# Attention inside a fused attention and MoE kernel: both key tiles kept apart in the first 16 units, and x divided by the softmax sums in place of the weights

## The chip, the cores and the metric

The kernel runs on one core of one Trainium2 chip. The metric is the device time of one launch in microseconds (us). The kernel before took 806.68 us (median of three runs, 804.89 to 807.85).

## The reference

Windowed attention with four sink keys, then a gated two-layer MLP ("MoE" in the names) over all tokens:

```
scores = q @ k.T / sqrt(64);  keep = (key < n_sink) or (0 <= query - key < window)
a = softmax(where(keep, scores, -1e9));  a = exp(s - max) / (sum + 1e-9)
x = (a @ v) gathered over 8 heads                      # 3072 tokens x 512
out = (sigmoid(x @ w_gate) * (x @ w_val)) @ w_out      # 512 -> 1536 -> 512
```

Batch 4, 8 heads, 768 tokens, head size 64; n_sink is 4 and window is 128, read at run time; the MoE weights come as float64 and are decoded on the chip into a high and a low float32r part.

## The kernel before

Attention runs in 96 units. A unit is one head of one batch over T = 2 query tiles of 128 tokens; units 0 to 7 are the heads of tiles 0 and 1 of batch 0, units 8 to 15 those of tiles 2 and 3, and so on. With a window of 128, a query tile sees the key tile before it and its own, and the four sink keys; the k array holds, after each 128 keys, the four sink keys again (KW = 132 columns per key tile). The first 16 units (`u < PLAIN`, L31) multiply in plain float32 from the loaded q, k and v; the others split their operands into high and low parts.

A unit before (`attend`, L691): TensorE (PE) makes the scores of a query tile, 132 columns for tile 0 and 260 for the rest: the key tile before, sinks, own key tile (`qk`, L733). VectorE (DVE) merges the two key tiles by COPY_PREDICATED with a triangle mask, since of each pair of keys 128 apart a query uses exactly one (`top`, L742), and makes the masked, negated scores and their minimum in one custom instruction over 132 columns. ScalarE (ACT) takes exp with the row sum (`exp`, L750). Then the sum gets 1e-9 (`guard`), its reciprocal is taken, the 128 weights of a row are multiplied by it on whichever of POOL (GpSimd), ACT or DVE the planner picks (L772), and the four sink weights go, multiplied, into `psk` (L791). PE transposes the merged weights (`turn`, L809), ACT copies them to SBUF, and two AFFINE_SELECTs on POOL unmerge them into two key tiles (`split`, L815). PE multiplies with v (`pv`, L871). After eight heads `join` (L927) adds the sink part (`sk`, `vsp`) to x and splits x into XH and XL, on which the MoE part (`feed_part`, L1090) works.

The order of every engine's instructions is written by a planner (`Plan.run`, L287): an event simulation with a cost in ns per operation, priorities (unit number; MoE matmuls have a late one), buffers per tag, and due times for the 36 weight decodes (L1160). Where PE has nothing ready before 130 us of the planner's time and its activity is under a floor, the planner puts a filler matmul (`warm`, L648, identity times identity, 128 columns, into m0); in the trace this is `m<-ident`. What is planned is a fixed order: on the chip each engine goes through it in line, and fillers are executed whether or not PE has to wait.

Of the kernel before, what the change touches and what calls it, by code (L numbers as in the profile page):

```python
# [20 lines left out]
NS = 4  # L21
# [411 lines left out]
def kernel(  # L433
# [124 lines left out]
    assert NR == 32  # L558
    VSP = Fixed(const.tile([3 * NR, H // 2, 2 * D], F32R, name="vsp"))
# [6 lines left out]
    VAL, MASKS, IDENT = Fixed(val), Fixed(am), Fixed(ident)  # L566
    nums = tile([128, 10], I32, "nums", 1)
# [59 lines left out]
    def later_masks():  # L627


        rel, relm, inm = mk()[:, 0:128], mk()[:, 432:560], mk()[:, 560:688]  # L630
        snk, inp = mk()[:, 400 : 400 + NS], mk()[:, 688 : 688 + NS]
        V.tensor_scalar(out=inm, in0=relm, scalar1=win, scalar2=None, op0=ALU.is_lt)
        V.tensor_scalar(
            out=inp, in0=rel[:, 0:NS], scalar1=128.0, scalar2=win, op0=ALU.add, op1=ALU.is_lt
        )
        V.tensor_tensor(out=inp, in0=snk, in1=inp, op=ALU.is_gt)
        for i, x in ((1, inp), (2, snk)):
            low(am[i][:, 0:128], inm)
            low(am[i][:, 128:KW], x)

# [16 lines left out]
    plan.op(0, [("V", 1200, later_masks)], [VAL, mk], [(MASKS, 1), (MASKS, 2)])  # L657
# [32 lines left out]

    def attend(u, b, h, t0, T, XR, XS, PSK):  # L691
# [7 lines left out]
        plain = u < PLAIN  # L699
# [4 lines left out]
        load(u, b, h, t0, T, prev, L, vraw, qkT, plain)  # L704
        kk2, qq2 = [(qkT, 0), (qkT, 4)], [(qkT, 2), (qkT, 6)]
        if plain:
            pairs = ((qT, kTf),)
            qk_reads, qk_ns = [qkT], 4
        else:
            qs = tile([128, W], F32R, "qs", BUFS["qs"])  # L710
            kh = tile([128, L * KW], F32R, "kh", BUFS["kh"])
            kl = tile([128, L * KW], F32R, "kl", BUFS["kh"])
            copy(u, W, qs, qT, qq2, [qs])
            copy(u, L * KW, kh, kTf, kk2, [kh])
            rest(
                u, W, lambda: qs()[D:128], lambda: qT()[D:128], lambda: qs()[D:128],
                qq2 + [qs], [qs],
            )
            rest(u, L * KW, kl, kTf, kh, kk2 + [kh], [kl])
            pairs = (qs, kh), (qs, kl)  # L720
            qk_reads, qk_ns = [qs, kh, kl], 2

        if h == 0:
            PSK[0] = tile([128, T, H, NS], F32, "psk", BUFS["psk"])
# [3 lines left out]
        for t in range(T):  # L728
            sc = tile([128, 512], F32, "a", BUFS["a"], ps)
            first = t0 + t == 0  # L730
            n = KW if first else KW + 128

            def qk(t=t, sc=sc, n=n):  # L733
                s0 = max(t + prev - 1, 0) * KW
                K = D if plain else 128
                for i, (qq, kk) in enumerate(pairs):
                    PE.matmul(
                        sc()[:, 0:n], lhsT=qq()[0:K, t * 128 : t * 128 + 128],
                        rhs=kk()[0:K, s0 : s0 + n], start=i == 0, stop=i == len(pairs) - 1,
                    )  # L740
# [14 lines left out]

            plan.op(u, [("PE", 10 + qk_ns * mac(n), qk)], qk_reads, [sc, (P, t)], busy=0.5 if plain else 0.9)
# [34 lines left out]
        def sink_weights(E):  # L791
            return lambda: E.tensor_tensor(
                out=psk()[:, 0:T, h], in0=P()[:, 0:T, 128:KW],
# [10 lines left out]
        Z = 1 if plain else 2  # L804
        wt = tile([128, 2, T, 2, 128], F32 if plain else F32R, "wt", BUFS["w"])
        w = lambda: wt()[:, 0:Z]
# [8 lines left out]
        def split():  # L815
            f = 1 - prev
            if T > f:
                G.affine_select(
                    out=w()[:, :, f:T, 0], in_=f32(w())[:, :, f:T, 1],
                    pattern=[[0, Z], [0, T - f], [-1, 128]], compare_op=ALU.is_gt, fill=0.0,  # L820
# [4 lines left out]
                pattern=[[0, Z], [0, T], [1, 128]], compare_op=ALU.is_ge, fill=0.0, base=0,  # L825
# [7 lines left out]
        if not plain:  # L833
            plan.op(
                u, [("V", vec(W), lambda: V.tensor_tensor(
                    out=w()[:, 1, :, 1], in0=tpv(), in1=w()[:, 0, :, 1].bitcast(F32),
                    op=ALU.subtract,
                ))],
                [tp, (wt, 0)], [(wt, 1)],
            )  # L840
        plan.op(u, [("G", 1100.0 if plain else 1400.0, split)], [], [wt])

        if plain:
            vhl = vraw
        else:
            vhl = tile([128, L, 2 * D], F32R, "vhl", BUFS["vhl"])
            copy(u, L * D, lambda: vhl()[:, :, 0:D], vraw, [vraw], [(vhl, 0)])
            rest(
                u, L * D, lambda: vhl()[:, :, D : 2 * D], vraw, lambda: vhl()[:, :, 0:D],
                [vraw, (vhl, 0)], [(vhl, 1)],  # L850
            )

        acc = None if plain else tile([128, 512], F32, "a", BUFS["a"], ps)
# [3 lines left out]
        if plain and h % 2 == 0:  # L857
            XR[0] = tile([128, 512], F32, "a", BUFS["a"], ps)
        xr = XR[0]
        M = D if plain else 2 * D  # L860


        blocks = []
        for l in range(L):
            tl = l - prev
            n = 128 if (tl < 0 or tl == T - 1) else 256
            blocks.append((-n, l, max(tl, 0) * 128, 0 if tl < 0 else tl * 256 + 128, n))
        blocks.sort()
        assert blocks[0][-1] == W

        def pv():  # L871
            a = (xr()[e : e + D] if plain else acc())[:, 0 : Z * W].rearrange("p (z x) -> p z x", z=Z)
# [8 lines left out]
        if plain:  # L881
            plan.op(
                u, [("PE", sum(5 + 4 * n / 2.4 for *_, n in blocks), pv)], [vhl, wt], [(xr, h % 2)]
            )
            if h % 2:
                plan.op(
                    u, [("A", act(W, True), lambda: A.copy(out=xs()[:, c], in_=xr()[:, 0:W]))], [xr],
                    [(xs, (c, 0)), (xs, (c, 1))],
                )
        else:  # L890
            low = tile([D, W], F32, "low", BUFS["small"])
            plan.op(
                u, [("PE", sum(mac(2 * n) for *_, n in blocks), pv)],
                [vhl, wt], [acc, low, (xs, (c, h % 2))],
            )
            plan.op(
                u, [("A", act(W, True), lambda: A.copy(out=low(), in_=acc()[D:128, 0:W]))], [acc], [low]
            )
            if u < ADDG:
                low2 = tile([D, W], F32, "low2", BUFS["small"])  # L900
                plan.op(
                    u, [("A", act(W, True), lambda: A.copy(out=low2(), in_=acc()[0:D, 0:W]))], [acc],
                    [low2],
                )
                plan.op(
                    u, [("G", pool(W), lambda: G.tensor_tensor(
                        out=low(), in0=low2(), in1=low(), op=ALU.add
                    ))],
                    [low2], [low],
                )  # L910
            else:
                plan.op(
                    u, [("V", vec(W), lambda: V.tensor_tensor(
                        out=low(), in0=acc()[0:D, 0:W], in1=low(), op=ALU.add
                    ))],
                    [acc], [low],
                )
            plan.op(
                u, [("V", vec(W), lambda: V.tensor_tensor(
                    out=xs()[e : e + D, c], in0=acc()[0:D, W : 2 * W], in1=low(), op=ALU.add  # L920
                ))],
                [acc, low], [(xs, (c, h % 2))],
            )
        if h == H - 1:
            join(u, b, t0, T, XS, psk)

    def join(u, b, t0, T, XS, psk):  # L927
# [3 lines left out]
        sk = tile([3 * NR, W], F32R, "sk", BUFS["sk"])  # L931

        def turn():
            for t in range(T):
                PE.transpose(
                    out=ts()[0:NR, t * 128 : t * 128 + 128],
                    in_=psk()[:, t].rearrange("p h s -> p (h s)"), identity=ident,
# [13 lines left out]
        )  # L951
        runs = [[0]]
# [5 lines left out]
        for i, xs in enumerate(XS):  # L958
# [15 lines left out]
            )  # L974
            for run in runs:
# [191 lines left out]
    for b in range(B):  # L1167
        t0 = 0
        for T in AT[b]:
            XR, XS, PSK = [None], [], [None]  # L1170
            for h in range(H):
                attend(u, b, h, t0, T, XR, XS, PSK)
# [81 lines left out]
```

## Time and profile before

| | |
|---|---|
| median of the runs | 806.68 us |
| the profiled execution's own time | 806.56 us |
| its span, first to last instruction | 804.9 us |
| PE busy | 787.0 us (98%) |
| DVE, ACT, POOL busy | 511.5, 415.7, 437.5 us |
| DMA | 94.35 MB, mean 117 GB/s |

Matmuls are pipelined and their ends are modelled, so one row's duration overlaps the next row's start; what a matmul costs in a stream is read from start to start. A float32 matmul has two records in the trace, so the 108 fillers are 216 records. The page's busy share of PE holds the fillers, which do no work for the result.

### The profile page before, as it was taken

What the parts mean: (1) busy time and instruction counts of PE and PEld (TensorE: products, weight loads), DVE (VectorE), ACT (ScalarE), POOL (GpSimd) and SP (SyncE); (2) the same over time, 40 slices, a digit from 0 to 9 for tenths busy, and PEclk for the clock granted to TensorE, in tenths of its full rate; (3) what the DMA queues carried; (4) which work ended last, traced back from release to release, by engine and by line L of the source; (5) the groups of instructions that cost most, each with busy time, mean ns of one, the idle gap of its engine ahead of it and who ended that gap; (6) DMA issues with size and microseconds to landing.
All of it is one profiled execution on the core that took longest, in us unless ns stands there. A gap on an engine that the chain in (4) does not pass through costs nothing. (4 is left out here: it accounts for less than half of the span.)

```text
span 804.9 us, 14932 instructions
## 1 busy us (share of the span) xinstructions
PE 787.0 (98%) x4618; PEld 715.3 (89%) x4618; DVE 511.5 (64%) x1560; ACT 415.7 (52%) x1173; POOL 437.5 (54%) x609
## 2 busy tenths in 40 slices
PE   9999999998999999999999999999999999999995
PEld 6787888977999989999999999999999999999994
DVE  6587798989888898989971388885861321111110
ACT  4677778787777776767760157663740210011001
POOL 4475689887678776766762267673751221121111
PEclk9999999999999999999999999999999999999998
DMA  4657676774735443544541134353311121112111
GB/s 138 173 172 210 181 223 203 235 237 130 207 107 153 127 133 93 149 110 122 141 113 58 43 113 129 106 129 107 96 44 42 48 71 40 50 43 78 40 40 56
DMA packets 98422, 94.35 MB, mean 117 GB/s; under 512 B 43168, under 2 KB 77984, under 8 KB 98336
## 3 DMA queue, kind: packets, MB, share of 16 engines
q1 hardware_dynamic: 98336, 93.32, 40.7%
q8 instruction: 39, 0.64, 0.3%
q14 instruction: 47, 0.39, 0.2%
HBM read 83.85 MB, written 9.44 MB: 116 GB/s over the span
## 5 line engine op out<-in xcount | busy, mean ns | idle before, releaser
L487 POOL TENSOR_TENSOR gl<-th,gh 128x384 fp32r<-128x384 f32 (+1 forms) x72 | 69.4, 963 | 197.0 <-DVE gh L487 184.8
L487 DVE SCALAR_TENSOR_TENSOR th<-th,m 128x384 f32<-128x384 f32 (+1 forms) x108 | 54.4, 504 | 180.3 <-PE m L487 178.6
L487 ACT ACTIVATE th<-m 128x384 f32<-128x384 f32 (+1 forms) x108 | 48.9, 453 | 208.2 <-PE m L487 206.8
L487 POOL TENSOR_SCALAR_AFFINE_SELECT wt<-wt 128x512 fp32r<-128x512 f32 (+3 forms) x192 | 119.8, 624 | 45.9 <-DVE wt L487 27.7
L487 PE MATMUL m<-XH,wvh 128*128 128x384 f32 (+1 forms) x432 | 140.0, 324 | 0.3 <-ACT th L487 0.3
L487 PE MATMUL m<-XH,wgh 128*128 128x384 f32 (+1 forms) x432 | 139.8, 324 | 0.0
L487 PE MATMUL m<-XH,wvl 128*128 128x384 f32 (+1 forms) x432 | 137.4, 318 | 0.0
L487 PE MATMUL m<-XH,wgl 128*128 128x384 f32 (+1 forms) x432 | 137.4, 318 | 0.0
L487 PE MATMUL m<-XL,wgh 128*128 128x384 f32 (+1 forms) x432 | 137.3, 318 | 0.0
L487 PE MATMUL m<-XL,wvh 128*128 128x384 f32 (+1 forms) x432 | 137.3, 318 | 0.0
L487 PE MATMUL o<-woh,gh 128*128 128x512 f32 x276 | 113.0, 410 | 1.0 <-DVE total L1202 1.0
L487 PE MATMUL o<-woh,gl 128*128 128x512 f32 x276 | 109.7, 397 | 1.3 <-DVE gl L487 0.6
L487 PE MATMUL o<-wol,gh 128*128 128x512 f32 x276 | 108.9, 395 | 2.0 <-DMA wol<-wol_d 2.0
L487 ACT ACTIVATE P<-P,negm_all 128x132 f32<-128x132 f32 x192 | 77.0, 402 | 31.5 <-DVE negm_all L487 28.7
L487 PEld LDWEIGHTS m<-XH,wvh 128*128 128x128 f32 x432 | 81.4, 188 | 3.3 <-issue 0.5
L487 PEld LDWEIGHTS m<-XH,wgh 128*128 128x128 f32 x432 | 81.5, 189 | 1.9 <-issue 0.3
L487 PEld LDWEIGHTS m<-XL,wgh 128*128 128x128 f32 x432 | 81.5, 189 | 1.5
L487 PEld LDWEIGHTS m<-XL,wvh 128*128 128x128 f32 x432 | 81.5, 189 | 1.4
L487 PEld LDWEIGHTS m<-XH,wvl 128*128 128x128 f32 x432 | 81.4, 188 | 0.0
L487 PEld LDWEIGHTS m<-XH,wgl 128*128 128x128 f32 x432 | 81.4, 188 | 0.0
L487 DVE CUSTOM_DVE_ANT_0 P<-a,am 128x132 f32<-128x132 f32 x192 | 56.0, 294 | 16.7 <-PE a L487 7.6
L487 PEld LDWEIGHTS o<-woh,gl 128*128 128x128 f32 x276 | 52.1, 189 | 15.8 <-DVE gl L487 1.8
(114 smaller groups left out, 1657.2 us busy)
## 6 DMA issues: line engine op xcount, KB each, us to landing
wol<-wol_d SPq DMA_DIRECT2D x108, 256.0 KB, 2.8
qkT<-in_k_dram SPq DMA_DIRECT2D x120, 99.0 KB, 2.6
qkT<-in_q_dram SPq DMA_DIRECT2D x176, 64.0 KB, 2.5
wst<-in_moe_w_gate_dram SPq DMA_DIRECT2D x12, 512.0 KB, 4.2
wst<-in_moe_w_val_dram SPq DMA_DIRECT2D x12, 512.0 KB, 4.4
wst<-in_moe_w_out_dram SPq DMA_DIRECT2D x12, 512.0 KB, 3.7
vraw<-in_v_dram SPq DMA_DIRECT2D x64, 96.0 KB, 2.4
out_dram<-w SPq DMA_DIRECT2D x23, 256.0 KB, 2.3
```

Source lines behind the costliest of these rows:

```text
L487: return lambda *a, **kw: tc.keep_in_program_order(op(*a, **kw))
```

## The change

For units 0 to 15 a new function `attend_plain` takes the place of the plain branches of `attend`:

- The two key tiles of a query tile stay apart. The mask-and-minimum instruction and exp work on 260 columns (132 for tile 0), with masks `am2` that hold the triangle; they are made at the start by eight more DVE instructions. COPY_PREDICATED and the AFFINE_SELECTs of these units go.
- PE transposes both halves: one or two transposes per query tile in place of one; each query tile's result is copied by an instruction of its own, on ACT or DVE.
- The weights are not divided. The row sums of 8 heads are collected in `psk` (40 columns in place of 32), and the sink weights are copied there unscaled. In `join`, 1e-9 is added and the reciprocal taken once for all heads, the transposed reciprocals are copied to `rt` (8 x 256), and for each half of x PE spreads them over 64 rows per head with four float32 matmuls (`spread`), by which DVE multiplies x.
- The planner's costs for these float32 matmuls change: `60 + 0.97 * n` for a score matmul (before `10 + 4 * mac(n)`), `10 + n` per block of `pv` (before `5 + 4 * n / 2.4`).

```diff
+    def attend_plain(u, b, h, t0, T, XR, XS, PSK):
...
+            def top(t=t, sc=sc, n=n, m=m):
+                V.tensor_tensor_reduce(
+                    out=P[t]()[:, 0:n], in0=sc()[:, 0:n], in1=m()[:, 0:n], op0=ALU.add,
+                    op1=ALU.min, scale=-SCALE, scalar=3.0e38, accum_out=negm_all[:, u, t : t + 1],
+                )
+            def exp(t=t, n=n):
+                A.activation(
+                    out=P[t]()[:, 0:n], in_=P[t]()[:, 0:n], func=AF.Exp,
+                    bias=negm_all[:, u, t : t + 1], scale=-1.0,
+                    accum_out=psk()[:, t, NR + h : NR + h + 1],
+                )
...
+            plan.op(u, [("PE", 60 + 0.97 * n, qk)], [qkT], [sc, (TURN, 0)], busy=0.5)
...
+                for y in range(y0, 2):
+                    c = KW if y > y0 else 0
+                    PE.transpose(
+                        out=tp()[:, (2 * t + y) * 128 : (2 * t + y) * 128 + 128],
+                        in_=P[t]()[:, c : c + 128], identity=ident,
+                    )
...
+                def spread(i=i, rpv=rpv):
+                    for k in range(4):
+                        e = k % 2 * D
+                        PE.matmul(
+                            rpv()[e : e + D, k // 2],
+                            lhsT=ident[0:H, 4 * i + k : 4 * i + k + 1].to_broadcast([H, D]),
+                            rhs=rt(), start=True, stop=True,
+                        )
+                plan.op(u, [("PE", 4 * (10 + W), spread)], [rt, IDENT], [rp], busy=0.5)
+                plan.op(
+                    u, [("V", vec(2 * W), lambda rpv=rpv, xs=xs: V.tensor_tensor(
+                        out=xs(), in0=rpv(), in1=xs(), op=ALU.mult
+                    ))],
+                    [rp], [xs],
+                )
```

Where instructions moved, three places. First PE around the products with v (`vraw`) of units 4 and 5: in the order before, with the weights in tiles P, and `m<-ident` the fillers:

```order
L487 MATMUL a_430<-ident,P_362 128x128 x2
L487 MATMUL m_90<-ident 128x128
L487 MATMUL a_435<-qkT_303 128x132
L487 MATMUL a_443<-qkT_303 128x260
L487 MATMUL a_447<-ident,P_385 128x128 x2
L487 MATMUL m_90<-ident 128x128
L487 MATMUL a_456<-qkT_364 128x132
L487 MATMUL m_90<-ident 128x128 x2
L487 MATMUL a_470<-qkT_364 128x260
L487 MATMUL m_90<-ident 128x128 x3
L487 MATMUL a_487<-wt_437,vraw_403 64x256
L487 MATMUL a_487<-wt_437,vraw_403 64x128
```

The order now around the products of units 2 and 3, where the weights lie in the tiles kh and kl:

```order
L487 MATMUL m_90<-ident 128x128
L487 MATMUL a_339<-qkT_269 128x132
L487 MATMUL m_90<-ident 128x128 x4
L487 MATMUL o_353<-wt_342,vraw_302 64x256
L487 MATMUL o_353<-wt_342,vraw_302 64x128
L487 MATMUL o_357<-ident,kh_308 128x128
L487 MATMUL a_360<-qkT_269 128x260
L487 MATMUL o_357<-ident,kl_325 128x128 x2
L487 MATMUL m_90<-ident 128x128 x3
L487 MATMUL a_382<-qkT_282 128x132
L487 MATMUL m_90<-ident 128x128 x2
L487 MATMUL o_353<-wt_365,vraw_333 64x256
```

Fillers stand in both, and each unit has three transposes in place of two. Over the whole order there are 108 fillers before and 100 now (73 and 65 of them ahead of the first MoE matmul), 192 transposes of weights before and 216 now.

Second, PE at the first join (`psk` is turned, then the sink part is added), before:

```order
L487 MATMUL a_559<-ident,psk_246 32x128 x2
L487 MATMUL a_565<-qkT_450 128x260
L487 MATMUL a_570<-wt_527,vraw_494 64x256
L487 MATMUL a_570<-wt_527,vraw_494 64x128
L487 MATMUL m_90<-ident 128x128 x3
L487 MATMUL a_588<-qkT_450 128x260
L487 MATMUL m_90<-ident 128x128 x3
L487 MATMUL a_570<-wt_563,vraw_505 64x256
L487 MATMUL a_570<-wt_563,vraw_505 64x128
L487 MATMUL a_612<-sk_568,vsp 128x256 x2
L487 MATMUL a_617<-sk_568,vsp 128x256 x2
```

And now, where `low` holds the transposed reciprocals and the matmuls into 64x256 are `spread`:

```order
L487 MATMUL a_557<-ident,psk_239 40x128 x2
L487 MATMUL m_90<-ident 128x128 x4
L487 MATMUL a_575<-wt_537,vraw_516 64x256
L487 MATMUL a_575<-wt_537,vraw_516 64x128 x2
L487 MATMUL a_581<-sk_561,vsp 128x256 x2
L487 MATMUL a_589<-low_570,ident 64x256 x4
L487 MATMUL a_598<-sk_561,vsp 128x256 x2
L487 MATMUL m_90<-ident 128x128 x6
L487 MATMUL a_611<-low_570,ident 64x256 x4
```

Eight float32 matmuls of 256 columns have come in at each of the two joins of the plain units.

Third, DVE ahead of the first mask-and-minimum instruction (ISA), before and now (`vhl` holds the new masks `am2`, `am_86` is the mask of tile 0):

```order
L487 TENSOR_TENSOR wst_156<-wst_156 128x4
L487 TENSOR_SCALAR am_87<-wst_156 128x128
L487 TENSOR_SCALAR am_87<-wst_156 128x4
L487 TENSOR_SCALAR am_88<-wst_156 128x128
L487 TENSOR_SCALAR am_88<-wst_156 128x4
L487 ISA P_212,negm_all<-a_192,am_86 128x132
```

```order
L487 SCALAR_TENSOR_TENSOR vhl_203<-wst_156,am_87 128x128
L487 COPY vhl_203<-am_87 128x4
L487 TENSOR_SCALAR vhl_203<-wst_156 128x128
L487 TENSOR_TENSOR vhl_203<-vhl_203,am_87 128x128
L487 TENSOR_SCALAR am_88<-wst_156 128x128
L487 TENSOR_SCALAR am_88<-wst_156 128x4
L487 SCALAR_TENSOR_TENSOR vhl_210<-wst_156,am_88 128x128
L487 COPY vhl_210<-am_88 128x4
L487 TENSOR_SCALAR vhl_210<-wst_156 128x128
L487 TENSOR_TENSOR vhl_210<-vhl_210,am_88 128x128
L487 ISA kh_231,negm_all<-a_192,am_86 128x132
```

Eight instructions now stand ahead of the first softmax instruction on DVE.

## Rows read from the trace of the kernel before

**Rows 1.** Busy time in stretches of the span. Columns: from:to in us, length, then PE busy (x instructions), PE weight loads, DVE, ACT, POOL, granted TensorE clock, DMA share, GB/s.

```profile
0.00:25.00 25.00, 23.28 (x85) 17.43 (x85) 13.99 (x63) 10.70 (x31) 9.62 (x19) 1.00 0.50 141
25.00:52.00 27.00, 27.00 (x164) 20.15 (x163) 18.42 (x68) 20.22 (x56) 17.13 (x25) 1.00 0.59 170
52.00:95.00 43.00, 42.37 (x269) 34.13 (x269) 32.06 (x99) 31.71 (x80) 27.37 (x40) 1.00 0.72 208
95.00:200.00 105.00, 98.67 (x687) 89.02 (x688) 96.66 (x218) 81.54 (x193) 89.91 (x98) 1.00 0.67 201
200.00:420.00 220.00, 219.01 (x1375) 204.17 (x1374) 192.56 (x649) 158.21 (x499) 159.34 (x252) 1.00 0.49 132
420.00:795.00 375.00, 373.56 (x2042) 348.53 (x2041) 157.77 (x465) 111.53 (x315) 134.08 (x179) 1.00 0.24 70
```

**Rows 2.** PE in order of time, shortly before the first MoE matmul, and the transpose with which the second join begins. Columns: start, duration in us, operation, shape, count of records.

```profile
38.59 1.38 PE L487 MATMUL m<-ident 128*128 128x128 f32 x10
39.80 0.38 PE L487 MATMUL a<-ident,P 128*128 128x128 f32 x2
40.02 0.39 PE L487 MATMUL m<-ident 128*128 128x128 f32 x2
40.34 1.14 PE L487 MATMUL a<-qkT 64*128 64x260 f32 x4
41.41 1.38 PE L487 MATMUL m<-ident 128*128 128x128 f32 x10
42.63 0.38 PE L487 MATMUL a<-ident,P 128*128 128x128 f32 x2
...
50.59 1.60 PE L487 MATMUL m<-ident 128*128 128x128 f32 x12
51.96 0.36 PE L487 MATMUL m<-XH,wgh 128*128 128x256 f32 x1
...
89.73 0.38 PE L487 MATMUL a<-ident,psk 128*32 128x128 f32 x2 [0.64 <-DVE psk L487]
```

**Rows 3.** The same view a little later: the product with v of a unit with three key tiles (one matmul of 256 columns and two of 128, six records), the MoE matmul behind it, and two transposes with the MoE matmul behind them.

```profile
54.27 1.08 PE L487 MATMUL a<-wt,vraw 128*64 128x256 f32 x6
55.29 0.39 PE L487 MATMUL m<-XH,wvh 128*128 128x256 f32 x1
...
56.11 0.38 PE L487 MATMUL a<-ident,P 128*128 128x128 f32 x2
56.24 0.36 PE L487 MATMUL m<-XH,wgh 128*128 128x256 f32 x1
```

**Rows 4.** The same view near the start, with the time at which PE's pace changes.

```profile
5.36 3.30 PE L487 MATMUL a<-qkT 64*128 64x132 f32 x8 [0.17 <-DMA qkT<-in_q_dram]
...
12.54 1.67 PE L487 MATMUL a<-qkT 64*128 64x132 f32 x4
14.14 1.65 PE L487 MATMUL m<-ident 128*128 128x128 f32 x6
15.58 0.64 PE L487 MATMUL a<-ident,P 128*128 128x128 f32 x2
...
18.90 1.54 PE L487 MATMUL a<-wt,vraw 128*64 128x256 f32 x4
...
21.52 1.54 PE L487 MATMUL a<-wt,vraw 128*64 128x256 f32 x4
23.00 1.61 PE L487 MATMUL m<-ident 128*128 128x128 f32 x10
...
24.98 0.93 PE L487 MATMUL a<-qkT 64*128 64x132 f32 x4
25.84 0.49 PE L487 MATMUL m<-ident 128*128 128x128 f32 x2
```

**Rows 5.** Groups of instructions over the whole span, shapes kept apart. Columns: count, busy us, mean ns of one, idle time before them and what ended it.

```profile
L487 ACT ACTIVATE P<-P,negm_all 128x132 f32<-128x132 f32 x192 | 77.0, 402 | 31.5 <-DVE negm_all L487 28.7 <-POOL wt L487 0.9 <-DVE rs L487 0.8
L487 DVE CUSTOM_DVE_ANT_0 P<-a,am 128x132 f32<-128x132 f32 x192 | 56.0, 294 | 16.7 <-PE a L487 7.6 <-ACT wgh L487 1.3 <-DVE a L487 0.2
L487 ACT ACTIVATE P<-P,rs 128x128 f32<-128x128 f32 x125 | 46.3, 397 | 19.6 <-DVE rs L487 17.9 <-DVE bad L1188 0.8
L487 DVE COPY_PREDICATED a<-tri,a 128x128 f32<-128x128 int32 x160 | 45.6, 285 | 8.2 <-PE a L487 7.2 <-DVE rs L487 0.3
L487 PE MATMUL m<-ident 128*128 128x128 f32 x216 | 39.3, 318 | 2.3 <-POOL ident masks.py:199 1.4 <-ACT th L487 0.9
L487 DVE TENSOR_TENSOR xr<-a,xr 128x512 f32<-128x512 f32 x24 | 16.4, 685 | 2.9 <-PE a L487 2.6
L487 POOL TENSOR_SCALAR_AFFINE_SELECT wt<-wt 128x256 f32<-128x256 f32 x24 | 12.2, 507 | 5.1 <-ACT wt L487 4.0
L487 DVE RECIPROCAL rs<-rs 128x2 f32<-128x2 f32 x96 | 15.2, 159 | 7.1 <-POOL rs L487 5.6
L487 ACT COPY wt<-a 128x256 f32<-128x256 f32 x16 | 6.0, 375 | 3.8 <-PE a L487 3.6
```

**Rows 6.** DVE in order of time at the start: the last masks and the first mask-and-minimum instruction.

```profile
5.32 0.35 DVE L487 SCALAR_TENSOR_TENSOR wst<-wst,val 128x128 f32<-128x128 f32 x1
...
6.67 0.50 DVE L487 TENSOR_SCALAR am<-wst 128x128 f32<-128x128 f32 x4
7.08 0.29 DVE L487 CUSTOM_DVE_ANT_0 P<-a,am 128x132 f32<-128x132 f32 x1
```

More of the change, by code (lines that the diff above doesn't have):

```diff
@@ L566 @@
     VAL, MASKS, IDENT = Fixed(val), Fixed(am), Fixed(ident)
+    TURN = Fixed(None)
+    am2 = [None] + [tile([128, PW], F32, "vhl", BUFS["vhl"]) for _ in range(2)]
     nums = tile([128, 10], I32, "nums", 1)
@@ L703, in attend @@
         kTf = lambda: qkT()[:, W : W + L * KW]
-        load(u, b, h, t0, T, prev, L, vraw, qkT, plain)
+        load(u, b, h, t0, T, prev, L, vraw, qkT, False)
         kk2, qq2 = [(qkT, 0), (qkT, 4)], [(qkT, 2), (qkT, 6)]
[L706 to L721, printed above, removed]
+        qs = tile([128, W], F32R, "qs", BUFS["qs"])
+        kh = tile([128, L * KW], F32R, "kh", BUFS["kh"])
+        kl = tile([128, L * KW], F32R, "kl", BUFS["kh"])
+        copy(u, W, qs, qT, qq2, [qs])
+        copy(u, L * KW, kh, kTf, kk2 + [TURN], [kh])
+        rest(
+            u, W, lambda: qs()[D:128], lambda: qT()[D:128], lambda: qs()[D:128],
+            qq2 + [qs], [qs],
+        )
+        rest(u, L * KW, kl, kTf, kh, kk2 + [kh, TURN], [kl])
+        pairs = (qs, kh), (qs, kl)
         if h == 0:
-            PSK[0] = tile([128, T, H, NS], F32, "psk", BUFS["psk"])
+            PSK[0] = tile([128, T, NR], F32, "psk", BUFS["psk"])
         psk = PSK[0]
@@ L754, in exp @@
                 )
-            plan.op(u, [("PE", 10 + qk_ns * mac(n), qk)], qk_reads, [sc, (P, t)], busy=0.5 if plain else 0.9)
+            plan.op(u, [("PE", 10 + 2 * mac(n), qk)], [qs, kh, kl], [sc, (P, t)], busy=0.9)
             plan.op(
@@ L832, in attend @@
         )
[L833 to L853, printed above, removed]
+        plan.op(
+            u, [("V", vec(W), lambda: V.tensor_tensor(
+                out=w()[:, 1, :, 1], in0=tpv(), in1=w()[:, 0, :, 1].bitcast(F32),
+                op=ALU.subtract,
+            ))],
+            [tp, (wt, 0)], [(wt, 1)],
+        )
+        plan.op(u, [("G", 1400.0, split)], [], [wt])
+        vhl = tile([128, L, 2 * D], F32R, "vhl", BUFS["vhl"])
+        copy(u, L * D, lambda: vhl()[:, :, 0:D], vraw, [vraw], [(vhl, 0)])
+        rest(
+            u, L * D, lambda: vhl()[:, :, D : 2 * D], vraw, lambda: vhl()[:, :, 0:D],
+            [vraw, (vhl, 0)], [(vhl, 1)],
+        )
+        acc = tile([128, 512], F32, "a", BUFS["a"], ps)
         if h % 4 == 0:
@@ L856, in attend @@
         xs, c = XS[-1], h // 2 % 2
[L857 to L869, printed above, removed]
+        blocks = blocks_of(T, prev)
         def pv():
-            a = (xr()[e : e + D] if plain else acc())[:, 0 : Z * W].rearrange("p (z x) -> p z x", z=Z)
+            a = acc()[:, 0 : 2 * W].rearrange("p (z x) -> p z x", z=2)
             for i, (_, l, c0, r0, n) in enumerate(blocks):
@@ L880, in attend @@
         e = (h % 2) * D
-        if plain:
-            plan.op(
[L883 to L894, printed above, removed]
+        low = tile([D, W], F32, "low", BUFS["small"])
@@ new lines, in attend @@
+        plan.op(
+            u, [("PE", sum(mac(2 * n) for *_, n in blocks), pv)],
+            [vhl, wt], [acc, low, (xs, (c, h % 2))],
+        )
+        plan.op(
+            u, [("A", act(W, True), lambda: A.copy(out=low(), in_=acc()[D:128, 0:W]))], [acc], [low]
+        )
+        if u < ADDG:
+            low2 = tile([D, W], F32, "low2", BUFS["small"])
+            plan.op(
+                u, [("A", act(W, True), lambda: A.copy(out=low2(), in_=acc()[0:D, 0:W]))], [acc],
+                [low2],
@@ L895, in attend @@
             )
             plan.op(
-                u, [("A", act(W, True), lambda: A.copy(out=low(), in_=acc()[D:128, 0:W]))], [acc], [low]
-            )
[L899 to L917, printed above, removed]
+                u, [("G", pool(W), lambda: G.tensor_tensor(
+                    out=low(), in0=low2(), in1=low(), op=ALU.add
+                ))],
@@ L924, in attend, with join @@
         if h == H - 1:
             join(u, b, t0, T, XS, psk)
-    def join(u, b, t0, T, XS, psk):
+    def join(u, b, t0, T, XS, psk, plain=False):
         W, g, vs = T * 128, b * NT + t0, VSP
@@ L931, in join @@
         sk = tile([3 * NR, W], F32R, "sk", BUFS["sk"])
+        nr = NR + H if plain else NR
         def turn():
@@ L951, in join @@
         )
+        if plain:
+            rt = tile([H, W], F32, "low", BUFS["small"])
+            plan.op(
+                u, [("A", act(W, True), lambda: A.copy(out=rt(), in_=ts()[NR:nr, 0:W]))], [ts], [rt]
+            )
         runs = [[0]]
```

145 lines of the change are left out of this document (129 added, 16 removed).

## The prediction, made before the changed kernel was run

> **What bounds the kernel now.** I read the busy times by stretch first [rows 1]. From 200 to 795 us PE is busy for 592.6 of 595 us: whatever is late at 200 us is late at the end, and whatever has come earlier is gained. So the change, which ends in the second join at about 95 us, is worth what it does to the time at which PE is through with the attention of units 0 to 15 and the MoE matmuls that lie between. Two stretches come before that. From 95 to 200 us DVE is busy for 96.7 of 105 us and POOL for 89.9, with most of the weight decodes in them, and PE idles 6.3 us. From 0 to 95 us DVE has 64.5, ACT 62.6 and POOL 54.1 us of work: none of them is full.
>
> The question is then what sets the pace of the first 95 us, and the order of PE in time answers it [rows 2]. From 25 to 52 us PE is busy for 27.00 of 27 us [rows 1], and that is not waiting in disguise: five fillers from 38.59 to 39.80 us are 0.242 us apart, five from 41.41 to 42.63 us 0.244, six from 50.59 to 51.96 us 0.228. If PE waited for a transpose's weights, the fillers ahead would be through sooner or the last would be stretched unevenly. The planner put a filler wherever it thought PE idle, but its costs for the other engines are long, so on the chip they are ready when PE comes. In the first 95 us PE's own line, fillers included, is the bound. The reader is to see that an engine with 16% of its work in fillers can still be the one that everybody waits for.
>
> **The change part by part.** PE first, since its line is the sum.
>
> Spread: 16 float32 matmuls of 256 columns, eight per join. No row has this shape. The nearest is the product with v, also float32 into 64 partitions: 512 columns in 55.29 - 54.27 = 1.02 us, 2.0 ns a column [rows 3], so 0.51 us each and 8.2 us in all. The score matmuls agree: two of 260 columns take 41.41 - 40.34 = 1.07 us [rows 2]. That they read 8 rows and not 128 should not matter, as 64 rows (scores) and 128 (products) cost the same by column. The planner reckons 4 * 266 = 1.06 us for four of them, where the rows say 2.04. Upper end 8.6 us (score rate), lower end half, 4.1 us, if two that write different halves of the partitions could run together; I take 8.2, the row.
>
> The Trainium skill has a rule that speaks for the lower end ("TensorE: Matmul & The Clock Gate", Part 3, on packing small matmuls): matmuls placed on different column groups of the array can be in flight at the same time, and three of them gave 2.38 times the speed there. The four of a spread alternate between partitions 0 and 64, so by it the sum would be some 4 us lower. In this trace no two neighbours write different halves, so it shows neither.
>
> Transposes: 24 more (216 for 192). Two take 0.22 us ahead of a filler [rows 2] and 0.13 us ahead of an MoE matmul [rows 3]: 1.6 to 2.6 us, I take 2.1.
>
> Fillers: 8 fewer (100 for 108) at 0.242 us [rows 2]: -1.9 us. In the trace they are the 216 records of the group [rows 5]. Up to about 23 us, where PE runs at half pace, both orders hold about as many, so the full-pace price stands.
>
> Scores and products with v keep their number and shapes: 0. That the planner now thinks them nearly half as long (a score matmul of 260 columns 312 ns, where the row has 535) makes it believe PE idle too early; it only moves them, and the fillers it adds for that are in the count.
>
> So PE's line gets longer by 8.2 + 2.1 - 1.9 = 8.4 us.
>
> The other engines lose work. DVE: 24 COPY_PREDICATED at 285 ns, 6.8 us, and 16 reciprocals at 159 ns, 2.5 us [rows 5]; it gains 128 columns in 24 mask-and-minimum instructions (0.13 us each by the slope between 132 columns, 294 ns, and 512 columns, 685 ns [rows 5]), 3.2 us, four multiplications of x at 685 ns, 2.7 us, and the masks. POOL loses 24 selects at 507 ns, 12.2 us [rows 5], and the eight smaller ones of tile 0. ACT, POOL and DVE together lose 32 scalings (397 ns on ACT, at most 12.7 us) and gain 16 copies of at most 375 ns and 24 longer exps (402 ns before; the same 0.13 us more, 3.1 us). All of this lies beside PE's line in a stretch where the three are two thirds busy; I cost it at nothing. If that cover were gone, the extra DVE and ACT work would cost up to 6 us, and the removed work would give back more: that is the first rival.
>
> Masks: the eight new DVE instructions stand ahead of the first mask-and-minimum instruction, which starts at 7.08 us; one of 128x128 with three inputs takes 0.35 us and four plain ones start to start 0.41 us [rows 6], so eight take at most 2.8 us. Behind it waits exp, then PE's first transpose. But PE now has 784 columns of scores (4.1 ns a column at half pace: 392 in 14.14 - 12.54 us [rows 4]) and six fillers ahead of that transpose, 3.2 + 2.9 = 6.1 us from its first score at 5.36 us [rows 4], until 11.5; DVE is through with the first mask at 7.08 + 2.8 + 0.3 = 10.2 and ACT at 10.6. Cost 0; uncovered 2.8 us. (A filler at half pace is 0.48 us: three from 14.14 to 15.58 us [rows 4].)
>
> Join: reciprocal, turn, copy to `rt`, spread, multiplication now stand between `psk` and XH, some 3 us more of a chain. PE fills it with six fillers, the other spread, transposes and scores, and the MoE work that is issued by the product of unit 17 is the same in both orders (174 matmuls into m, 30 into o). Cost 0; uncovered up to 3 us a join.
>
> Against this, waits of PE may shrink. What can go is the 0.6 us of idle before 95 us and the 6.3 us to 200 us [rows 1]; the latter follow DVE's work on decodes and on units 16 and up, which the change leaves (12 of 36 decodes stand ahead of the 32nd mask-and-minimum instruction before, 13 now), but PE arrives later at it. Between 0 and 7 us, I take 2.5.
>
> Sum: 8.4 - 2.5 = +5.9 us on the profiled execution's 806.56 us (0.12 us under the median of the runs): 812.5 us.
>
> **The rivals.**
>
> One, faster: the other engines set the pace of the first 95 us and PE's even fillers deceive me. Then a unit's chain loses a reciprocal (0.16 us), a scaling (0.40) and two selects (1.01) [rows 5], some 1.6 us; with two units in flight that is 0.8 us a unit, 12.5 us in 16 units, and PE's 8.4 us lie partly in its waits. 806.6 - 12.5 = 794, with half of the PE work paid 798 us. For it: 18 of 63 fillers are gone by the product of unit 7. Against it: 27.00 of 27 us. It decides if PE is seen to wait between fillers.
>
> Two, no change: the spreads run in pairs. 4.1 + 2.1 - 1.9 - 2.5 = +1.8, 808.4 us. For it nothing but the alternating halves; against it that no row shows such an overlap.
>
> Three, slower still: PE stays at half pace longer. At 12.54 us 392 score columns took 1.60 us, at 24.98 us 0.86 [rows 4]; the granted clock reads 1.00, the upper level of 2.4 GHz, in both stretches [rows 1], so the pace is read from the starts. Ahead of the rise PE ran two products and fillers without a score matmul between (18.90 to 23.00 us). In the new order scores and transposes stand between, and the next such run (four fillers and a product) comes some 8 us later: each us costs half, +4 us, 816.5 us.
>
> **How the numbers follow.** Forecast 0.50, faster 0.17, paired spreads 0.20, late clock 0.13. The likeliest is 812.5 us, its own range 809 to 816 (spreads at 8.2 to 8.6, transposes 1.6 to 2.6, waits 0 to 5.5). The range of 8 in 10 is 803 to 819 us: below it lies most of rival one, above it a late clock with an uncovered join. Half a per cent, 4 us, is about what a measurement of this kernel can tell from no change. Faster by more than that (under 802.6): rival one, 0.17. Within: rival two and the low end of the forecast, 0.20 + 0.08. Slower (over 810.7): the rest of the forecast and rival three, 0.42 + 0.13 = 0.55.
>
> **What would show it.** Right: spreads 0.5 us apart, 1.0 us for two; fillers still evenly 0.24 us apart between 25 and 50 us; the second `psk` transpose, at 89.73 us before [rows 2], some 5 to 9 us later; DVE, ACT and POOL less busy before 95 us with no gain from it; from 200 us on as before. Wrong: a second `psk` transpose before 88 us (rival one), spreads 0.25 us apart (two), score matmuls at 4 ns a column after 25 us (three), or a middle stretch (the first split score to the last decode) that got shorter by more than 5 us, since then the other engines' order, which I took as unchanged there, decided.

## The result, and the profile after

The changed kernel took 809.59 us (median) against 804.89 us for the kernel before: the ratio is 1.0065 with a 95% interval of 1.0039 to 1.0090, that is 5.2 us slower (3.1 to 7.2; the two medians differ by 4.7). Of the 13 executions three lie far above the others (816, 830 and 1006 us), where all 70 of the kernel before stayed under 809 us; none of the three was profiled, and this ratio and those below leave out executions more than 1.5% above the quickest of their kernel.

The profiled execution took 809.59 us, its span is 807.8 us. The page's line of busy times of the changed kernel:

```profile
PE 791.2 (98%) x4658; PEld 716.3 (89%) x4658; DVE 511.8 (63%) x1538; ACT 407.6 (50%) x1160; POOL 426.4 (53%) x574
```

Busy times by stretch of the changed kernel, with the columns of [rows 1]:

```profile
0.00:25.00 25.00, 23.42 (x83) 16.63 (x83) 10.03 (x57) 8.72 (x24) 6.24 (x17) 1.00 0.48 139
25.00:52.00 27.00, 26.41 (x158) 18.50 (x157) 17.10 (x52) 16.20 (x47) 11.12 (x15) 1.00 0.53 146
52.00:95.00 43.00, 42.93 (x268) 32.95 (x267) 33.64 (x70) 25.28 (x66) 22.35 (x25) 1.00 0.64 183
95.00:200.00 105.00, 99.51 (x705) 90.31 (x704) 97.48 (x224) 85.25 (x198) 88.48 (x93) 1.00 0.71 213
200.00:420.00 220.00, 218.26 (x1378) 203.63 (x1377) 190.07 (x644) 150.45 (x478) 156.83 (x235) 1.00 0.48 130
420.00:795.00 375.00, 374.99 (x2054) 350.21 (x2053) 162.51 (x492) 119.96 (x346) 140.38 (x191) 1.00 0.26 73
```

Up to 95 us DVE has 60.8 us of work where it had 64.5, ACT 50.2 for 62.6, POOL 39.7 for 54.1 [rows 1], and PE is as full as before. PE in order of time, changed kernel: a unit's transposes and score matmul, and what stands around the joins:

```profile
26.21 0.86 PE L487 MATMUL o<-wt,vraw 128*64 128x256 f32 x4
27.01 0.33 PE L487 MATMUL o<-ident,kh 128*128 128x128 f32 x1
27.27 0.70 PE L487 MATMUL a<-qkT 64*128 64x260 f32 x2
27.90 0.44 PE L487 MATMUL o<-ident,kl 128*128 128x128 f32 x2
28.18 0.83 PE L487 MATMUL m<-ident 128*128 128x128 f32 x6
...
46.19 0.38 PE L487 MATMUL a<-ident,psk 128*40 128x128 f32 x2
...
48.05 1.08 PE L487 MATMUL a<-wt,vraw 128*64 128x256 f32 x6 [0.59 <-DVE negm_all L487]
49.07 0.50 PE L487 MATMUL a<-sk,vsp 96*128 96x256 f32 x2
49.50 1.08 PE L487 MATMUL a<-low,ident 8*64 8x256 f32 x8
50.51 0.51 PE L487 MATMUL a<-sk,vsp 96*128 96x256 f32 x2
50.85 1.50 PE L487 MATMUL m<-ident 128*128 128x128 f32 x12
52.29 1.08 PE L487 MATMUL a<-low,ident 8*64 8x256 f32 x8
53.30 0.44 PE L487 MATMUL a<-ident,kh 128*128 128x128 f32 x2
...
94.63 0.38 PE L487 MATMUL a<-ident,psk 128*40 128x128 f32 x2
```

The second `psk` transpose comes at 94.63 us, 4.9 later than in [rows 2]. The loss stays: the 50th matmul of woh by gl starts at 214.68 us before and at 219.94 us now (+5.3), the 280th of 288 at 784.42 and 789.82 us (+5.4). Only in its last microseconds does this execution of the kernel before lose time: its last matmuls start 0.42 us apart, those of the changed kernel 0.23 us, so the two spans differ by 2.9 us (804.9 and 807.8). Four spreads take 50.51 - 49.50 = 1.01 us, half of what the forecast has. A unit's three transposes take 0.26 us (one, 27.01 to 27.27) and 0.28 us (two, 27.90 to 28.18), where a unit's two took 0.22 us [rows 2]; and a score matmul between them takes 0.63 us, where two in a row took 0.535 us each [rows 2].

An account of PE, each row counted from its start to the next row's start, up to the tenth matmul of woh by gl (107.09 us before, 112.77 us now, each the start of the row behind it; a wait of PE is counted with the row ahead of it):

| us | before | after | difference |
|---|---|---|---|
| spreads | 0 | 4.03 | +4.03 |
| transposes of weights | 4.47 | 8.72 | +4.25 |
| score matmuls, units 0 to 15 | 19.21 | 20.91 | +1.70 |
| fillers | 33.10 | 29.88 | -3.22 |
| products with v, units 0 to 15 | 15.82 | 15.15 | -0.67 |
| all else | | | -0.41 |
| sum | | | +5.68 |

### The profile page after: what moved, and what is told of

Its sections match the earlier page's. It is cut to its first block, busy times and chain, and to the rows that moved or that the text cites. A ratio compares the mean times of both kernels' runs of the same rounds, so it can differ in the third digit from the quotient of the medians.

```text
span 807.8 us, 14953 instructions
## 1 busy us (share of the span) xinstructions
PE 791.2 (98%) x4658; PEld 716.3 (89%) x4658; DVE 511.8 (63%) x1538; ACT 407.6 (50%) x1160; POOL 426.4 (53%) x574
## 5 line engine op out<-in xcount | busy, mean ns | idle before, releaser
L487 POOL TENSOR_SCALAR_AFFINE_SELECT wt<-wt 128x512 fp32r<-128x512 f32 (+1 forms) x160 | 107.5, 673 | 38.1 <-DVE wt L487 29.2
L487 ACT ACTIVATE P<-P,negm_all 128x132 f32<-128x132 f32 x160 | 64.3, 402 | 20.6 <-DVE negm_all L487 17.2
L487 PEld LDWEIGHTS o<-woh,gl 128*128 128x128 f32 x276 | 51.8, 188 | 13.5 <-POOLq L1335 0.9
L487 PEld LDWEIGHTS o<-wol,gh 128*128 128x128 f32 x276 | 52.0, 188 | 10.3 <-DMA wol<-wol_d 4.9
```

Of the source, the lines that this page charges most:

```text
L487: return lambda *a, **kw: tc.keep_in_program_order(op(*a, **kw))
```

## The experiments

**What the spreads cost: left out.**

```diff
-                    for k in range(4):
+                    for k in range(0):
...
-                    u, [("V", vec(2 * W), lambda rpv=rpv, xs=xs: V.tensor_tensor(
-                        out=xs(), in0=rpv(), in1=xs(), op=ALU.mult
-                    ))],
+                    u, [("V", vec(2 * W), lambda: None)],
```

> The changed kernel without the 16 spread matmuls and without the multiplication of x by the reciprocals, in the same order otherwise; it leaves out the division by the softmax sums in units 0 to 15. If PE's line sets the pace of the first 95 us, the span falls by what the spreads take from start to start in the changed kernel, 4.0 us (two spreads of four in 1.0 us each per join), to 803 to 806 us. If the other engines or the join's chain set it, the DVE multiplications and the longer chain go too, and the span falls by 0 to 1 us where PE is not the bound, or by more than 6 us where the chain is.

Measured: 807.98 us, ratio to the kernel before 1.0033 (1.0016 to 1.0050). Its profiled execution has another history of pace at the start than the changed kernel's: a score matmul of 132 columns at 5.4 us takes 0.30 us, where the changed kernel's takes 0.57, and half pace lies between about 12 and 18 us. So I compare with the next run, which has the same history (by itself it is worth 2.2 us at the tenth matmul of woh by gl, 110.36 us there for 112.54 in the changed kernel): the tenth matmul is 1.7 us earlier, not 4. The rest stands as two waits of 1.1 us each that the next run doesn't have, for DVE's xr and for ACT's weights. Its list of waits of PE up to 120 us has (waited for, us, times, longest):

```profile
PE a L487 <- DVE xr L487: 1.1, 2, 0.8
PE a L487 <- ACT P L487: 1.1, 1, 1.1
```

So PE's line is the bound, but the other engines are only about 2 us behind it.

**Two spreads at a time? Another order of the halves.**

```diff
-                    for k in range(4):
+                    for k in (0, 2, 1, 3):
```

> The changed kernel with the four matmuls of a spread in the order 0, 2, 1, 3, so that two neighbours write the same half of the partitions and only the middle pair writes different halves. If neighbours on different halves run together, four take about three matmuls' time, 1.5 us in place of 1.0, and the 16 spreads 6.0 us in place of 4.0. If a spread matmul is cheap for another reason (8 rows of input in place of 64 or 128), four still take 1.0 us from start to start.

Measured: 808.4 us in a single execution; four spreads take 1.02 us. By the sum alone I took this to speak against pairs. The view of single records says otherwise. A narrow stretch of PE's order in time, first of the changed kernel, up to just behind the start of the first spread and then 0.2 us into it:

```profile
49.50 0.42 PE L487 MATMUL a<-low,ident 8*64 8x256 f32 x1
...
49.50 0.43 PE L487 MATMUL a<-low,ident 8*64 8x256 f32 x2
```

and 0.1 us into the spreads in this run's order:

```profile
50.10 0.44 PE L487 MATMUL a<-low,ident 8*64 8x256 f32 x2
```

Two records of 0.42 us lie within 0.43 us and 0.44 us: they run side by side in both orders. In the changed kernel the eight records of four spreads start in four pairs, 0.01 us apart within a pair, at 49.50, 49.77, 49.98 and 50.20 us. The first matmul of a product with v, whose neighbours write the same half, shows one record at a time: its two start at 48.05 and 48.32 us. The order of issue doesn't prevent the overlap, so this run's total couldn't decide. A record doesn't say which half it writes; that a pair is two matmuls into different halves is inferred here, and the run with wide spreads below tests it.

**Number of rows, and the form of the stationary.** Four runs asked whether a spread is cheap because few rows are read, or because one column is read 64 times.

```diff
-                            lhsT=ident[0:H, 4 * i + k : 4 * i + k + 1].to_broadcast([H, D]),
+                            lhsT=ident[0:nr, NR + 4 * i + k : NR + 4 * i + k + 1].to_broadcast([nr, D]),
```

> The changed kernel with the spread matmuls reading 40 rows in place of 8 (the transposed sink weights stand in the first 32, and the matching rows of the identity's column are zero, so the same numbers come out). The run with the halves in another order showed four spreads in 1.0 us whatever half they write, so it is not running together that makes them cheap. If it is the 8 rows, four now take about 2.0 us, the price of a value product by column. If it is the 64 columns of the stationary operand that repeat, or the place of the spreads in the order, four still take 1.0 us.

```diff
+            plan.op(u, [("V", vec(W), lambda: V.memset(rt(), 0.0))], [], [rt])
...
+                            lhsT=ident[:, NR + 4 * i + k : NR + 4 * i + k + 1].to_broadcast([128, D]),
```

> The changed kernel with the four spreads of a half reading all 128 rows (a tile cleared by one DVE instruction per join, the reciprocals in rows 32 to 39, and whole columns of the identity) in place of 8. The products with v, at 2.0 ns a column, read 128 rows into 64 partitions; the scores, at the same pace, 64 rows into 128 partitions; the spreads so far 8 or 40 rows into 64 partitions, so both numbers were 64 or fewer for them alone. If it is that both numbers are small that halves the price, the four spreads now take about 2.0 us; if it is the column that is repeated 64 times, or something else, 1.0 us as before.

```diff
+                            lhsT=rep[0:H, k] if 4 * i + k < 2 else ident[0:H, 4 * i + k : 4 * i + k + 1].to_broadcast([H, D]),
```

> The changed kernel with the stationary of heads 0 and 1 written out as 64 real columns by a DVE copy, for the first two of the four spreads of a join's first half; the other six keep the one column read 64 times. If reading one column 64 times is what makes a spread cheap, the first four of a join take 0.5 + 0.5 + 0.25 + 0.25 = 1.5 us and the second four 1.0; if not, 1.0 us for both.

```diff
+                            lhsT=rep[:, k] if 4 * i + k < 2 else ident[:, NR + 4 * i + k : NR + 4 * i + k + 1].to_broadcast([128, D]),
```

> Both at once: 128 rows, and written-out columns for heads 0 and 1, so that the first two spreads of a join have the form of a product with v. If rows or columns decide alone, this agrees with the run that showed it; if each alone changes nothing and both together do, the first four take 1.5 us and the second four 1.0; if all stay at 1.0 us, neither is the reason and what sets the products with v apart lies elsewhere (their sums run over several matmuls).

Measured: four spreads take 1.01 us in each of the four (the first kernel took 807.91 us in all). The 128-row run, and the one with written-out columns, PE in order of time:

```profile
54.61 1.08 PE L487 MATMUL a<-low,ident 128*64 128x256 f32 x8
55.62 0.51 PE L487 MATMUL a<-sk,vsp 96*128 96x256 f32 x2
```

```profile
68.55 0.65 PE L487 MATMUL a<-low,rep 8*64 8x256 f32 x4
69.03 0.60 PE L487 MATMUL a<-low,ident 8*64 8x256 f32 x4
69.56 0.51 PE L487 MATMUL a<-sk,vsp 96*128 96x256 f32 x2
```

Neither the rows nor the form of the stationary matters for the overlap. But the last three took 818.53, 828.94 and 835.92 us, far above their small edits. Each of the three was executed once, all on one chip that none of the experiments above used; the kernel before took 806.62 us there, also once. Up to the first join their PE order is the changed kernel's (but for the name of two spreads). Here is PE in order of time around 20 us, of the changed kernel and then of the run with written-out columns:

```profile
19.36 1.54 PE L487 MATMUL o<-wt,vraw 128*64 128x256 f32 x4
20.83 0.48 PE L487 MATMUL o<-ident,kh 128*128 128x128 f32 x1
21.10 0.49 PE L487 MATMUL o<-ident,kl 128*128 128x128 f32 x2
21.51 0.49 PE L487 MATMUL a<-qkT 64*128 64x132 f32 x2
21.93 0.71 PE L487 MATMUL m<-ident 128*128 128x128 f32 x4
```

```profile
19.36 1.54 PE L487 MATMUL o<-wt,vraw 128*64 128x256 f32 x4
20.84 0.48 PE L487 MATMUL o<-ident,kh 128*128 128x128 f32 x1
21.11 0.64 PE L487 MATMUL o<-ident,kl 128*128 128x128 f32 x2
21.67 0.81 PE L487 MATMUL a<-qkT 64*128 64x132 f32 x2
22.41 1.22 PE L487 MATMUL m<-ident 128*128 128x128 f32 x4
```

To 20.84 us they agree within 0.02 us. Then the first goes over to full pace and the second doesn't: it has 82 records of PE from 25 to 52 us, where the changed kernel has 158, is busy for 27.00 of 27 us at it, and comes to full pace at 64 us. Its second `psk` transpose is at 113.67 us, 19 us later. The 128-row run comes to full pace at 36 us, the one with both edits at 64 us like this one. That is what the third rival feared, a late rise, at a price of 19 us here. That the new order brings it is not shown: the same order rose at 21 us in the changed kernel's profile, and a part of the chip in it is not excluded.

**More fillers at the rise, and spreads that take both halves.**

```diff
+        made[0] += 1
+        for _ in range(5 if made[0] == 18 else 1):
...
+                        n = 2 * D if (i, k % 2) == (0, 0) else D
...
-                            rpv()[e : e + D, k // 2],
+                            rpv()[e : e + n, k // 2],
```

> The changed kernel with four more fillers in one place, behind the three that start at 17.8 us (ahead of the second product with v), and, apart from that, with a stationary of 128 columns in place of 64 for two of the four spreads of a join's first half (their upper 64 rows are written again by the next spread). Fillers: the runs of the 128-row and written-out spreads have PE's instructions in the changed kernel's order up to the first join, and PE stays at half pace there until 36 to 64 us, where the changed kernel's profile has the rise at 21 us. Theory: the order is thin around 20 us and meets the rise by a narrow margin; then a longer stretch without score matmuls makes the rise sure, the profile shows full pace at about 22 us, the executions of 814 us and more, some one in four of the changed kernel's kind so far, do not come, and the median is 0 to 2 us above 809.6 (four fillers of 0.24 to 0.48 us). Rival: the half pace has another cause than the order; then such executions come as before, and one in four lies above 814 us. Spreads: if 64 columns of stationary are what makes a spread cheap, the four with two of 128 columns take 1.5 us and the second four 1.0; if not, 1.0 us.

Measured: 822.57 us, ratio 1.0215 (1.0173 to 1.0257). PE at the two joins of this run, where the first row is a narrow stretch 0.26 us into the first wide spread:

```profile
51.44 0.48 PE L487 MATMUL a<-low,ident 8*128 8x256 f32 x1
...
51.44 2.46 PE L487 MATMUL a<-low,ident 8*128 8x256 f32 x8
53.82 0.50 PE L487 MATMUL a<-sk,vsp 96*128 96x256 f32 x2
...
111.99 2.46 PE L487 MATMUL a<-low,ident 8*128 8x256 f32 x8
114.38 0.51 PE L487 MATMUL a<-sk,vsp 96*128 96x256 f32 x2
```

With two of the four wide, no two of the eight records start as a pair any more, and all four go one behind the other: 2.38 us, 0.60 us each, at both joins. A narrow one by itself takes 0.57 us (52.06 to 52.63). This settles the spreads: one costs what the forecast said or a little more, and two into different halves run at once. For the fillers the run is inconclusive. The rise came at about 23 us (expected 22), but behind the wide spreads PE fell to half pace at 54.2 us, by its stretches:

```profile
40.00:48.00 8.00, 8.00 (x48) 5.63 (x48) 4.64 (x14) 4.34 (x13) 2.78 (x5) 1.00 0.48 150
48.00:56.00 8.00, 7.41 (x41) 5.31 (x40) 5.70 (x11) 5.48 (x12) 3.29 (x5) 0.89 0.52 156
56.00:64.00 8.00, 8.00 (x30) 5.32 (x30) 3.76 (x7) 1.69 (x4) 2.21 (x2) 0.50 0.28 98
```

and again at 115.6 us, behind the second join's. Every execution took over 818 us; only one was profiled, so it is not shown that the fall is the cause in the others. The two edits should not have been in one kernel; whether a surer rise takes the scatter away stays open.

**What the fillers are for.** Every second one left out behind the 40th, in the changed kernel:

```diff
+            n += o is None
+            if o is not None or n <= 40 or n % 2:
+                fn()
```

> The changed kernel with every second filler left out after the 40th (30 of 100), everything else in the same order. If PE's line with its fillers is the bound, each is worth 0.242 us: 7.3 us less, 801 to 804 us, as long as PE's clock stays up. If the other engines set the pace, PE waits where the fillers stood and the time stays within 1 us. If the clock falls back, scores take 4 ns a column again somewhere after 25 us, and the time rises.

Measured: 816.32 us, ratio 1.0101 (1.0062 to 1.0140), an interval in which the changed kernel's 1.0065 lies. Of six executions (808.6 to 957.8 us) none gave back the 7.3 us. In the profiled one (825.32 us) PE is busy nearly throughout, at a granted clock of 0.50 (the level of 1.2 GHz) from 16 us until past 56 us:

```profile
16.00:24.00 8.00, 8.00 (x25) 5.20 (x25) 0.99 (x5) 3.15 (x10) 1.65 (x3) 0.50 0.35 104
...
40.00:48.00 8.00, 8.00 (x24) 4.82 (x23) 1.28 (x6) 2.99 (x10) 3.27 (x4) 0.50 0.32 92
56.00:64.00 8.00, 7.82 (x29) 4.88 (x27) 1.58 (x3) 2.88 (x9) 1.45 (x2) 0.58 0.30 75
64.00:72.00 8.00, 7.44 (x49) 4.91 (x50) 6.56 (x14) 6.57 (x16) 4.46 (x5) 1.00 0.65 205
```

This can't be laid to the missing fillers. The fortieth filler starts at 51.8 us there, so no filler is missing before that, and PE has been at half pace since about 12 us; it is the late rise of the run with written-out columns, which has all its fillers, over again. So the run shows that nothing came back, and not what a filler does for the pace. In the other direction, all 35 behind the first MoE matmul left out:

```diff
+            if o is not None or n <= 65:
```

> The changed kernel without its last 35 fillers, those behind the first MoE matmul, all else in the same order. If PE's line is the bound there too, 35 times 0.242 us go: 8.5 us less, 800 to 802 us. If the other engines are close behind, part comes back as waits: 803 to 807 us. If the clock falls back for it, it is slower than the changed kernel.

Measured: 810.88 us, ratio 1.0066 (1.0043 to 1.0090): no change against the changed kernel. Ten fillers, 2.4 us, are gone ahead of the second `psk` transpose, which comes at 92.68 us, 1.95 us earlier than in the changed kernel (0.35 us of that is there at the first join already): up to there PE's line is most of the bound. Up to the tenth matmul of woh by gl 26 are gone, 6.1 us, and PE reaches it at the same time (112.65 us for 112.54). PE has waited 2.3 us more by then, and from 95 to 113 us its granted clock is 0.81, where the changed kernel has 1.00. Further on it waits longer for the weights wol. Waits from 50 to 200 us, of this run and then of the changed kernel:

```profile
PE o L490 <- DMA wol<-wol_d: 5.8, 5, 2.0
```

```profile
PE o L487 <- DMA wol<-wol_d: 2.7, 2, 1.7
```

The gain went into waits and into a lower clock, so behind 95 us PE's line is not the only bound.

**The planner's costs put back.**

```diff
-            plan.op(u, [("PE", 60 + 0.97 * n, qk)], [qkT], [sc, (TURN, 0)], busy=0.5)
+            plan.op(u, [("PE", 10 + 4 * mac(n), qk)], [qkT], [sc, (TURN, 0)], busy=0.5)
...
-            u, [("PE", sum(10 + n for *_, n in blocks), pv)], [vraw, wt], [(xr, h % 2)]
+            u, [("PE", sum(5 + 4 * n / 2.4 for *_, n in blocks), pv)], [vraw, wt], [(xr, h % 2)]
```

> The changed kernel with the planner's costs of the float32 score and value matmuls as they were before the change (10 + 4 mac(n), 5 + 4 n / 2.4): the planner writes another order, with 56 fillers in place of 100 (41 of them ahead of the first MoE matmul, before 65). If PE's line is the bound, 44 fillers at 0.242 us are 10.6 us, so 797 to 801 us and faster than both kernels. If the other engines set the pace, the time stays at 808 to 811 us with PE waiting for them in the first 95 us; if the clock rises later for the fewer fillers, 801 to 806 us.

Measured: 807.66 us, ratio 1.0047 (1.0022 to 1.0071), between the outcomes that were stated. PE is at half pace until about 36 us: a score matmul of 132 columns at 33.38 us lasts 0.81 us, one of 260 columns at 37.38 us 0.70 us. Up to the tenth matmul of woh by gl it has 8.6 us less of fillers than the changed kernel, but 2.2 us more of scores, 2.7 of products and 1.1 of transposes, and it is there 3.3 us earlier: most of what the fillers save goes back as pace.

**The transposes alone**, as dummies in the kernel before:

```diff
+                if plain and t0 + t:
+                    PE.transpose(
+                        out=tp()[:, 256 + t * 128 : 384 + t * 128], in_=P()[:, t, 0:128],
+                        identity=ident,
+                    )
```

> The kernel before with 24 more transposes in its plain units, one per query tile but the first, into PSUM columns that nobody reads; order, fillers and all else as before. If PE's line sets the pace, 24 times 0.11 to 0.18 us come on top: 2.6 to 4.3 us, 807.5 to 809.2 us where the kernel before has 804.9. If the other engines set it, no change.

Measured: 807.53 us, ratio 1.0024 (1.0008 to 1.0040), so +2.2 us (805.32 us before). They stand beside other transposes here, and cost 3.1 us by the account up to the tenth matmul of woh by gl; in the changed order, where more of them stand apart, 4.25.

**DVE loaded up**, a test of the first rival:

```diff
+                if n == PW:
+                    V.tensor_copy(out=P[t]()[:, 0:256], in_=sc()[:, 0:256])
```

> The changed kernel with a copy of 256 columns from PSUM in front of each of the 24 wide mask-and-minimum instructions, on DVE, in the same order; its output is overwritten at once. About 0.3 us each, 7 to 8 us of DVE work in the first 95 us, about what the change took off the DVE with the COPY_PREDICATEDs. If PE's line sets the pace, the time rises by less than 2 us. If DVE does, it rises by 7 us, to 816 us.

Measured: 809.76 us, ratio 1.0060 (1.0034 to 1.0086), the changed kernel's time with 69.3 us of DVE up to 95 us in place of 60.8. DVE is not the bound there; ACT and POOL were not loaded in this way.

## Why the prediction was right, and where its steps failed

The forecast was 812.5 us in a range of 803 to 819, slower by 5.9; it is 809.59 us, slower by 5.2. (The forecast started from the profiled 806.56 us, 1.7 us above the 804.89 of all runs.) The mechanism held: PE's line with its fillers paces the first 95 us, what it loses there stays, and the work taken from DVE, ACT and POOL gave nothing. The ballast run, the added transposes and the run without spreads show it, with two limits: taking the spreads out gave back 1.7 us of 4, so the other engines are close, and of 6.1 us of late fillers nothing came back. PE's fillers weigh more than the prediction says: up to 95 us they take 30.3 us of PE's line in the kernel before, from start to start, a third and not 16%.

The sum was right by luck, by errors that cancel:

- **Spreads, 8.2 us forecast, 4.0 measured.** The step that failed is "0.51 us each and 8.2 us in all": one costs 0.57 us by itself, but two into different halves of the partitions run together. That was the lower bound and the second rival, whose mechanism is right. The rule of the Trainium skill ("TensorE: Matmul & The Clock Gate", Part 3) that matmuls on different column groups can be in flight at once agrees with the trace here: two at a time, 1.01 us for four, against 2.38 us where a wide one keeps them apart.
- **Transposes, 2.1 us forecast, 4.25 measured.** I priced 24 instructions by rows in which two stand together. In the new order they stand in groups of one to four between other work. At full pace a lone one takes 0.26 us, two take 0.14 us ahead of an MoE matmul and up to 0.31 ahead of a score matmul, four take 0.44 to 0.59; the 24 added ones cost 0.18 us each where the forecast had 0.09.
- **Scores and products, 0 forecast, +1.7 and -0.7 measured.** Same number and shapes, but scores of 260 columns stand more often alone between other work, at 0.63 us for 0.535. The products got cheaper by their place: at half pace one of 384 columns takes 1.47 us and at full pace 0.80 (two at half pace before, at 18.90 and 21.52 us [rows 4], one now, at 19.36 us).
- **Fillers, -1.9 us forecast, -3.2 measured.** Of this 0.5 us is waits behind fillers, which the next point counts too. The rest is 0.35 us for each of eight, between the price at full pace, 0.24, and at half pace, 0.48 [rows 4]; the forecast took all at full pace, but five of the eight went ahead of 25 us (27 fillers there before, 22 now).
- **Waits of PE, -2.5 us forecast.** By the stretches PE idles 2.35 us up to 95 us before and 2.24 now, and from 95 to 200 us 6.3 before and 5.5 now: 0.9 us less, not 2.5. (From 200 us on it idles 2.4 us before and 1.8 now.)
- **Masks and joins, 0:** PE's waits up to 95 us include 0.6 us for the minima (`negm_all`), at the first join, and none for masks.

The second rival's 808.4 us is nearer to the measured time (1.2 us off) than the forecast (2.9), but by the difference, +1.8 against +5.2 measured, the forecast's +5.9 is the nearer one. For the spreads the rival's mechanism was the true one; its sum had the transposes too low and the scores at nothing. The third rival, a late clock, did not set the median, but such executions exist: with the same order PE stayed at half pace until 36 us or past 60 us in four profiled ones (the three above and the one with half the fillers), 9 to 26 us slower than the changed kernel, where I had put 4 us. Whether the order, the chip or something else brings them is open; 3 of 13 executions of the changed kernel took over 814 us and none of the 12 without spreads. The first rival, other engines, fell.

## What to carry to other kernels

Price an added matmul by what stands around it: a transpose alone ahead of a score matmul cost 0.26 us where two ahead of a filler cost 0.22, and two narrow matmuls into different halves cost one. Don't book fillers that an edit sheds as time won: in none of the three kernels with fewer fillers did their time come back in full, and pace and waits took the rest. With one and the same order PE came to full pace at 21, 36 or 64 us, so look at the pace of the start in every profile before two of them are compared.

## What the runs showed of the hardware that was not expected

- Float32 matmuls with 64 stationary columns into different halves of the partitions overlap, in either order of issue: four of 256 columns in 1.01 us, the same with 8, 40 or 128 rows and with a repeated or a written-out column; 2.38 us when two of them are 128 columns wide.
- The same instructions, at the same times within 0.02 us, came to full pace at 21 us in one execution (of the changed kernel) and at 64 us in another (with written-out columns). In the second, the granted clock reads 1.00 from 25 to 52 us, although PE does half the work there; in the run with half the fillers it reads 0.50 at the same pace, from 40 to 48 us. Why the one execution rises and the other doesn't is open.
- Behind 2.38 us of wide spreads, which read 8 rows, PE fell to half pace at both joins (one profiled execution); behind 1.01 us of narrow ones in the changed kernel it didn't. That the wide spreads are the cause is not shown.
